# A fused attention and two-MLP kernel: sums of squares of the heads from one matmul pass instead of two, with squares paired across 64 partitions and stacked halves

## The chip, the cores and the metric

The kernel runs on one core of one Trainium2 chip. The metric is device time in microseconds (us). The engines are named as the profile names them: PE (matrix engine; PEld is its weight load), DVE (vector engine), ACT (scalar engine), POOL (GpSimd) and SP (the queue that issues all DMAs of this kernel).

## What is computed

The reference, cut to what matters:

```python
kv  = einsum('bhsd,bhse->bhde', k, v)            # 8 batches, 8 heads, 576 rows, head size 64
out = einsum('bhsd,bhde->bhse', q, kv)
rms = sqrt(mean(out * out, axis=-1) + 1e-06)     # over the 64 elements of one head
x   = out / rms * g_norm                         # -> 4608 tokens x 512
h   = x @ w_in                                   # 512 -> 2048
x   = (P(h) / (Q(h) + 1e-06)) @ w_out            # P cubic, Q quadratic in |h|; 2048 -> 512
y   = (silu(x @ w_gate) * (x @ w_val)) @ w_o2    # 512 -> 1536 -> 512
```

Everything is float32. The kernel gets float32 accuracy out of single-pass matmuls by splitting a factor into a rounded high part and the low rest.

## The kernel before

Tokens are worked on in nine tiles T = 0 to 8 of 512 tokens (`N`). Activations lie with features on partitions: one head pair (two heads of 64) fills 128 partitions, and four head pairs (`HP`) make the 512 features of a tile.

The first MLP is a loop over 144 steps s: nine tiles t of 16 slices f of the hidden layer. A step puts three kinds of work on PE: `h_mm(s)`, 12 matmuls of 512 columns (4 feature blocks, three products of high and low parts each, `mm3` on lines 112 to 114); `y_mm(s - 2)`, 12 matmuls of the second weight on the activation `ghl` of two steps before; and a piece of the attention of the next tile, `attn_pe(s)`. `g_step(s)` emits what the other engines do for a step: on ACT `e1`, `e2`, `e3` from the bank `ph`, then the high part of `ghl` of the step before, then two more functions of `e2`; on DVE two operations that finish the step before (`g_finish`), the products of this step, and at the end a list `lows` of subtractions that make low parts; on POOL the low part of `ghl`. `y_mm` begins with the high part and wants the low part at its second matmul (line 113).

The attention of tile T = t + 1 is spread over the 16 steps of tile t, four steps (phases 0 to 3, `ph` in the code) for each head pair. Phase 3 of the group before puts `out_mm` on PE (the output `po` in a bank). In phase 0 ACT squares `po` into `sq` (line 327). For T of 2 and more it also rounds the square to the high half of `sqhl` (line 330), and DVE subtracts at the end of the step to make the low half (put on the list by `attn_mid`). In phase 1, after `y_mm`, `ss_mm` sums the squares of each head over its partitions with a block matrix of ones: one matmul on the high half and one on the low half (lines 340 and 341). Phase 2 takes the reciprocal root on ACT and makes three DVE operations (`norm_ops`), phase 3 splits the result into `x` (ACT, then POOL). Tile T = 1 (worked on during t = 0) and tile T = 0 (worked on in a prologue ahead of the loop) use one unsplit matmul on line 338 instead.

Tiles T = 2 to 8 have 4 head pairs each: 28 groups of four steps, from about 143 to 790 us. After about 890 us the second MLP runs; it has no part in the change.

During the prologue and t = 0 the weights are fetched as 64-bit words and converted. `wa_fetch` takes one set per step: a slice of `w_in` and a slice of `w_out`, each 512 KB and one DMA (line 182), into one of two raw buffers that it takes in turn. `wa_scale` (ACT, end of a step) rescales both as soon as they have landed, DVE joins them in the next step, ACT and DVE split them, and the end of that frees the buffer for the fetch after the next. In the same steps SP issues the loads of k and v (`kv_load`) and of q. All instructions of an engine run in the order in which they are written (the schedule is written out by hand); DMAs are issued by SP in that order.

Of the kernel before, what the change touches and what calls it, by code (L numbers as in the profile page):

```python
# [8 lines left out]
F32 = mybir.dt.float32  # L9
F32R = mybir.dt.float32r  # L10
I32 = mybir.dt.int32
I64 = mybir.dt.int64
AF = mybir.ActivationFunctionType
ALU = mybir.AluOpType

P = 128
# [4 lines left out]
N = 512  # L21
# [3 lines left out]
HP = H // 2  # L25
# [16 lines left out]
def fused_kernel(ctx: ExitStack, tc: tile.TileContext, kv_main, kv_left, q_t, w_in, w_out, w_gate, w_val, w_o2, ab, g_norm, out):  # L42
# [13 lines left out]
    nc = tc.nc  # L56
# [15 lines left out]
    at_p = attn_ctx.enter_context(tc.tile_pool(name="attn", bufs=1, side="right"))  # L72
# [4 lines left out]
    ones = const.tile([P, P], F32R, name="ones")  # L77
    ones_f = const.tile([P, P], F32, name="ones_f")
    ones_b = const.tile([P, P], F32, name="ones_b")
    na = const.tile([P, 4], F32, name="na")  # L80
    rows = w_p.tile([1, 3, P], F32, tag="w3", name="rows")
# [7 lines left out]
    kvc = at_p.tile([P, B - 2, HP, D], F32, name="kvc")  # L89
    for n in (18, 20, 22, 24, 26, 28, 3):  # L90
        w_p.tile([P, 2, N], F32, tag=f"w{n}", name="place")
    kvf = w_p.tile([P, 2, HP, P], F32, tag="w31", name="kvf")

    def act(out, in_, func=AF.Copy, **kw):
        nc.scalar.activation(out=out, in_=in_, func=func, **kw)  # L95
# [34 lines left out]
    def w_exp(st):  # L130
        _, _, hf = w_views(st)
        act(hf, hf, AF.Prelu, scale=2.0 ** -112, alpha=-(2.0 ** 32))
# [33 lines left out]
    wa_src = [("i", f, w_in[f]) for f in range(LAG)]  # L166
    wa_sets = [(f,) for f in range(LAG)]
    for f in range(NF1):
        n = len(wa_src)
# [7 lines left out]
    def wa_fetch():  # L177
        if wa_n[0] < len(wa_sets):
            ns, (pool, tag) = wa_sets[wa_n[0]], wa_raw[wa_home[wa_n[0]]]
            r = pool.tile([P, 2 if tag in ("hl", "stg") else 1, N], I64, tag=tag, name="wraw")  # L180
            for j, n in enumerate(ns):
                nc.sync.dma_start(out=r[:, j, :], in_=wa_src[n][2])
            raws.append((ns, r[:, :len(ns), :].rearrange("p a n -> p (a n)")))
            wa_n[0] += 1

# [45 lines left out]
    st = {}  # L231
    segs = {}
    for t in range(TILES):
        t0, ss = t * N, []
        while t0 < (t + 1) * N:
            b = t0 // S
            n = min((b + 1) * S, (t + 1) * N) - t0
# [42 lines left out]
    def diag(j):  # L280
        return slice(64 * j, 64 * j + 64)

    def kv_evac_first(b, ps, hps):
        for j in range(2):
            dst, src = kvf[diag(j), b, hps, diag(j)], ps[diag(j), hps, diag(j)]
            act(dst, src)

    def kv_evac(n, k, ps):
        flat = kvc.rearrange("p b h d -> p (b h) d")
# [3 lines left out]
    def kv_split(b):  # L293
        hi, lo = kvh[b % 2], kvl[b % 2]
        ops = []
        for j in range(2):
            o = (diag(j), slice(0, HP), diag(j))
            src = kvf[diag(j), 1, :, diag(j)] if b == 1 else kvc[diag(j), b - 2, :, :]
            act(hi[o], src)
            ops.append(partial(sub, nc.vector if b < 3 else nc.gpsimd, lo[o], src, hi[o]))  # L300
        return ops

    def q_load(T, hp, pool=None, tag="q"):
# [21 lines left out]

    def square(T, ps):
        sq = at_p.tile([P, N], F32, tag="t1", name="sq")
        act(sq, ps, AF.Square)
        if T >= 2:
            hl = at_p.tile([P, 2, N], F32R, tag="hl", name="sqhl")  # L330
            act(hl[:, 0, :], sq)
            st["sql"] = (hl[:, 1, :], sq, hl[:, 0, :])
            return hl
        return sq

    def ss_mm(T, sq, ps):
        if T < 2:
            nc.tensor.matmul(ps, lhsT=ones_b, rhs=sq, start=True, stop=True)
        else:
            nc.tensor.matmul(ps, lhsT=ones, rhs=sq[:, 0, :], start=True, stop=False)  # L340
            nc.tensor.matmul(ps, lhsT=ones, rhs=sq[:, 1, :], start=False, stop=True)
        return ps

    def norm_start(T, pss, bufs=None):
# [5 lines left out]
    def norm_ops(ps, pss):  # L350
        r, u = st["n"]
        return [
            partial(stt, u, pss, D * EPS_RMS, u, ALU.add, ALU.mult),
            partial(stt, r, u, 3.0 * D, r, ALU.subtract, ALU.mult),
            partial(stt, u, ps, g_neg, r, ALU.mult, ALU.mult),
        ]

    def x_attn(T, hp, lo_eng, lows=None):
        if hp % 2 == 0:
            x_t[T, hp // 2] = x_p.tile([P, 2, 2, N], F32R, tag=f"x{T % 2}{hp // 2}", name="x")  # L360
        split(x_t[T, hp // 2][:, hp % 2, :, :], st["n"][1], lo_eng, lows)
# [12 lines left out]
    def at(c):  # L374
        T, f = divmod(c, NF1)
        i, ph = divmod(f, 4)
        return (T + 1, i, ph) if T + 1 < TILES else (None, None, None)

    def attn_head(c):

        T, i, ph = at(c)
        if ph == 0:
            st["sq"] = square(T, st["po"])
        elif ph == 2 and T >= 2:
            norm_start(T, st["ss"])

    def attn_start(c):
        T, i, ph = at(c)
        if T == 1 and ph == 1:
            norm_start(T, st["ss"])  # L390
        elif ph == 3 and T != 1:
            x_attn(T, i, nc.gpsimd)

    def attn_mid(c, lows):
        T, i, ph = at(c)
        if ph == 0 and T is not None and T >= 2:
            lows.append(partial(sub, nc.vector, *st["sql"]))
        elif T == 1 and ph == 2:
            x_attn(T, i, None, lows)
        return norm_ops(st["po"], st["ss"]) if ph == (1 if T == 1 else 2) else []  # L400

    def attn_tail(c):
        T, i, ph = at(c)
        if T is None:
            return
        f = c % NF1
        if c >= NF1 and f == 13 and T + 1 < B:
            run(kv_split(T + 1), 2)
        n = (T - 1) * HP + i + 1
        Tn, hp = n // HP + 1, n % HP  # L410
        if Tn < TILES:
            if ph == 0:
                q_load(Tn, hp)
            if ph == 2 and Tn > 1 and T > 1:
                q_split(Tn, hp)
# [44 lines left out]
    def run(ops, k=1):  # L460
        for op in ops[:k]:
            op()
        del ops[:k]

    def g_finish(s, ops, his=()):
        if s not in mid:
            return []
        e1, e2, e3 = mid.pop(s)
        stt(e1, e1, 1.0 + EPS_Q, e2, ALU.add, ALU.mult)
        stt(e3, e3, na[:, 0:1], e2, ALU.add, ALU.mult)  # L470
        run(ops, len(ops))
        w = s in WHOLE
        hl = g_p.tile([P, N] if w else [P, 2, N], F32 if w else F32R, tag="g", name="ghl")
        stt(hl if w else e3, e1, 2.0, e3, ALU.subtract, ALU.mult)
        lows = [hi() for hi in his[:1]]
        if not w:
            split(hl, e3, nc.gpsimd)
        hl_t[s] = hl
        return lows + [hi() for hi in his[1:]]

    def g_step(s, joins=(), his=(), exps=(), acts=()):
        ps = ew.pop(s)
        if s:
            attn_head(s)
        e1 = e_p.tile([P, N], F32, tag="e1", name="e1")
        e2 = e_p.tile([P, N], F32, tag="e2", name="e2")
        e3 = e_p.tile([P, N], F32, tag="e3", name="e3")
        act(e1, ps, AF.Square)
        act(e2, ps, AF.Abs, scale=ab_raw[:, 4:5])
        act(e3, ps, AF.Identity, scale=na[:, 3:4], bias=na[:, 2:3])  # L490
        if not s:
            attn_head(s)
        for r in exps:
            w_exp(r)
        attn_start(s)
        lows = [op for a in acts for op in a() or ()]
        ops = list(joins)
        lows = g_finish(s - 1, ops, his) + lows
        run(ops, len(ops))
        ops = attn_mid(s, lows)  # L500
        if s < NF1:
            run(ops)
        stt(e1, e1, b_abs[:, 1:2], e2, ALU.mult, ALU.add)
        act(e2, e1, AF.Abs_reciprocal_sqrt, bias=bias_q)
        act(e2, e2, AF.Square)
        nc.vector.tensor_tensor(out=e3, in0=e3, in1=ps, op=ALU.mult)
        run(ops)
        stt(e3, e3, na[:, 1:2], ps, ALU.add, ALU.mult)
        run(ops, len(ops))
        run(lows, len(lows))  # L510
        mid[s] = (e1, e2, e3)
# [527 lines left out]
    with tc.manual_schedule():  # L1039
# [8 lines left out]
        for i in range(HP):  # L1048
            kv_load(1)
            q_load(0, i, w_p, f"w{20 + i}")  # L1050
            if i == 0:
                nc.sync.dma_start(out=rows[:, 0, :], in_=g_norm.rearrange("(o p) -> o p", o=1))
                nc.sync.dma_start(out=rows[:, 2, :6], in_=ab.rearrange("(o p) -> o p", o=1))
            elif i == 1:
                wa_fetch()
# [4 lines left out]
        nc.vector.memset(rows[:, 1, :], 1.0)  # L1060
        nc.vector.memset(kvf, 0.0)
        nc.vector.memset(ones_b, 0.0)
        for j in range(2):
            nc.vector.memset(ones_b[diag(j), diag(j)], 1.0)
        nc.vector.memset(bias_q, 1.0 + EPS_Q)
        nc.vector.tensor_copy(out=ones, in_=ones_b)
        for i in range(2):
# [138 lines left out]
        for s in range(S1):  # L1206
# [62 lines left out]
            if t == TILES - 1:  # L1269
# [12 lines left out]
                elif 8 <= f < 12:  # L1282
                    k, c = divmod(f - 8, 2)
# [82 lines left out]
        for j in range(UP):  # L1366
            f, n = UP + j, 12 + 10 * j
# [19 lines left out]
        for n, i in enumerate(made):  # L1387
            at = (
# [3 lines left out]
            )[n % 3]  # L1392
# [88 lines left out]
```

## Time and profile before

| | before |
|---|---|
| time, median of 3 runs | 1680.99 us (1679.74 to 1682.69) |
| span of the profiled execution | 1678.3 us |
| PE busy | 1666.0 us (99%) |
| DVE busy | 1371.2 us (82%) |
| ACT busy | 1073.6 us (64%) |
| POOL busy | 473.1 us (28%) |
| granted TensorE clock, mean | 1.000 |

The span runs from the first to the last instruction of the profiled execution; its time by the clock of the runs is not told, and the median of the runs lies 2.7 us above the span. Busy time counts what an engine executes; it is not idle between overlapping matmuls. The TensorE clock was granted in full in every slice of the span.

### The profile page before, as it was taken

To read this page: it belongs to the slowest core of one execution; us is meant where nothing else is said; L and a number is where in the kernel's file an instruction comes from. 1 tells how busy PE (TensorE), PEld (TensorE's weight loads), DVE (VectorE), ACT (ScalarE), POOL (GpSimd) and SP (SyncE) were. 2 spreads that over 40 slices of the span, in tenths; PEclk is the share of its full clock that TensorE was granted. 3 is DMA by queue.
4 is the path that set the end of the run, shared out by engine and by line. 5 is a ranking of instruction groups with operands and counts; after the bars stand their busy time and mean duration, and the time that the engine had idled before them with its cause. 6 is when DMAs were issued, how large, how long until landed. Compare 5 with 4: busy or idle time off the path is not lost.

```text
span 1678.3 us, 24096 instructions
## 1 busy us (share of the span) xinstructions
PE 1666.0 (99%) x9040; PEld 1415.8 (84%) x9040; DVE 1371.2 (82%) x1913; ACT 1073.6 (64%) x1801; POOL 473.1 (28%) x331
## 2 busy tenths in 40 slices
PE   8999999999999999999999999999999999999999
PEld 5777888888888888888888888888888889999999
DVE  7999999999999999998996766778568859776665
ACT  7898888788788787877775444445435455444442
POOL 2112333333333343333330112223202155222221
PEclk9999999999999999999999999999999999999999
DMA  8861011011111110111425237243494354434431
GB/s 338 319 240 50 8 51 63 26 57 44 57 39 69 45 63 20 45 57 63 151 75 182 82 107 281 64 144 107 152 334 151 130 176 144 164 133 151 151 129 61
DMA packets 77850, 198.18 MB, mean 118 GB/s; under 512 B 6947, under 2 KB 35876, under 8 KB 75044
## 3 DMA queue, kind: packets, MB, share of 16 engines
q1 hardware_dynamic: 77732, 196.64, 33.3%
q8 instruction: 71, 1.16, 0.3%
q14 instruction: 47, 0.39, 0.1%
HBM read 130.02 MB, written 66.06 MB: 117 GB/s over the span
## 4 chain that ended last, share of the span: by engine, by line
PE 92%; DVE 4%; ACT 2%; DMA 2%; issue 1%; POOL 0%; SPq 0%; DVEq 0%; POOLq 0%; ACTq 0%
PE pb L112 10%; PE pb L113 10%; PE pb L114 10%; PE y L113 7%; PE ph L113 7%; PE ph L114 7%; PE ph L112 7%; PE y L114 7%; PE y L112 7%; PE pb L948 5%; PE pb L947 5%; PE pb L946 5%; DVE e L108 1%; ACT e L95 1%; DMA wraw<-in_w_in 1%
## 5 line engine op out<-in xcount | busy, mean ns | idle before, releaser
L98 POOL TENSOR_TENSOR ghl<-e,ghl 128x512 fp32r<-128x512 f32 x141 | 183.3, 1300 | 499.4 <-ACT ghl L95 289.8
L112 PE MATMUL pb<-xc,wu 128*128 128x512 f32 (+1 forms) x804 | 303.9, 378 | 0.0
L113 PE MATMUL pb<-xc,wu 128*128 128x512 f32 (+1 forms) x804 | 303.8, 378 | 0.0
L114 PE MATMUL pb<-xc,wu 128*128 128x512 f32 (+1 forms) x804 | 303.8, 378 | 0.0
L95 ACT ACTIVATE e<-pb 128x512 f32<-128x512 f32 (+1 forms) x162 | 92.8, 573 | 238.0 <-PE pb L114 237.7
L108 DVE SCALAR_TENSOR_TENSOR e<-e,e 128x512 f32<-128x512 f32 x285 | 226.3, 794 | 12.0 <-ACT e L95 4.9
L515 DVE TENSOR_TENSOR e<-e,pb 128x512 f32<-128x512 f32 (+1 forms) x216 | 140.6, 655 | 114.4 <-PE pb L114 63.5
L112 PE MATMUL ph<-x,wt 128*128 128x512 f32 x576 | 226.5, 393 | 0.3 <-ACT x L95 0.3
L113 PE MATMUL ph<-x,wt 128*128 128x512 f32 x576 | 225.0, 391 | 1.8 <-POOL x L98 1.6
L114 PE MATMUL ph<-x,wt 128*128 128x512 f32 x576 | 224.7, 390 | 0.0
L113 PE MATMUL y<-ghl,wt 128*128 128x512 f32 x564 | 221.5, 393 | 3.0 <-POOL ghl L98 2.8
L112 PE MATMUL y<-ghl,wt 128*128 128x512 f32 x564 | 221.5, 393 | 0.0
L114 PE MATMUL y<-ghl,wt 128*128 128x512 f32 x564 | 219.9, 390 | 0.0
L947 PE MATMUL pb<-wo,xo 128*128 128x256 f32 x756 | 213.9, 283 | 0.0
L948 PE MATMUL pb<-wo,xo 128*128 128x256 f32 x756 | 213.9, 283 | 0.0
L946 PE MATMUL pb<-wo,xo 128*128 128x256 f32 x756 | 213.9, 283 | 0.0
L112 PEld LDWEIGHTS pb<-xc,wu 128*128 128x128 f32 x804 | 151.0, 188 | 28.6 <-ACT e L95 0.4
L114 PEld LDWEIGHTS pb<-xc,wu 128*128 128x128 f32 x804 | 151.0, 188 | 28.1
L113 PEld LDWEIGHTS pb<-xc,wu 128*128 128x128 f32 x804 | 151.0, 188 | 28.0
L95 ACT ACTIVATE xo<-graw 128x768 fp32r<-128x768 f32 x122 | 99.1, 840 | 109.3 <-issue 49.9
L95 ACT ACTIVATE e<-ph 128x512 f32<-128x512 f32 x144 | 85.8, 596 | 119.3 <-PE ph L114 118.4
L946 PEld LDWEIGHTS pb<-wo,xo 128*128 128x128 f32 x756 | 145.1, 192 | 0.1
(138 smaller groups left out, 3409.2 us busy)
## 6 DMA issues: line engine op xcount, KB each, us to landing
graw<-gd SPq DMA_DIRECT2D x36, 768.0 KB, 4.4
gd<-gout SPq DMA_DIRECT2D x96, 256.0 KB, 2.2
kvm<-in_kv_main SPq DMA_DIRECT2D x32, 512.0 KB, 7.1
yraw<-yd SPq DMA_DIRECT2D x22, 512.0 KB, 7.0
q<-in_q_t SPq DMA_DIRECT2D x36, 256.0 KB, 3.7
yd<-sb SPq DMA_DIRECT2D x18, 512.0 KB, 3.5
out<-sb SPq DMA_DIRECT2D x17, 512.0 KB, 3.0
wraw<-in_w_in SPq DMA_DIRECT2D x16, 512.0 KB, 4.3
```

Source lines behind the costliest of these rows:

```text
L95: nc.scalar.activation(out=out, in_=in_, func=func, **kw)
L98: eng.tensor_tensor(out=out, in0=a, in1=b.bitcast(F32), op=ALU.subtract)
L108: nc.vector.scalar_tensor_tensor(out=out, in0=in0, scalar=scalar, in1=in1, op0=op0, op1=op1)
L112: nc.tensor.matmul(ps, lhsT=wh, rhs=xh, start=first, stop=False, skip_group_check=more)
L113: nc.tensor.matmul(ps, lhsT=wh, rhs=xl, start=False, stop=False, skip_group_check=more)
L114: nc.tensor.matmul(ps, lhsT=wl, rhs=xh, start=False, stop=last, skip_group_check=more)
L515: eng.tensor_tensor(out=out, in0=a, in1=b, op=op)
L946: nc.tensor.matmul(ps, lhsT=x[:, 0, i, :], rhs=wh, start=start, stop=False, skip_group_check=not first)
L947: nc.tensor.matmul(ps, lhsT=x[:, 0, i, :], rhs=wl, start=False, stop=False, skip_group_check=not first)
L948: nc.tensor.matmul(ps, lhsT=x[:, 1, i, :], rhs=wh, start=False, stop=stop, skip_group_check=not first)
```

## The change

The feature order inside a head pair is changed from (head, 64 elements) to (half, head, 32 elements): partitions 0 to 31 hold the first half of head 0, 32 to 63 the first half of head 1, 64 to 95 the second half of head 0, 96 to 127 the second half of head 1. A square and the square 64 partitions above it then belong to the same head. For tiles T of 2 and more:

- `square` makes two ACT squares of 64 partitions each, both written to partitions 0 to 63, and a POOL addition of the two in place of the rounding.
- `square_hi`, called by the new `attn_late` after the last function of `e2` in the same step, rounds the 64-partition sum to the high half in partitions 0 to 63 of `sqhl`; DVE writes the low half to partitions 64 to 127 at the end of the step.
- `ss_mm` is one matmul over all 128 partitions.

The matrix of ones follows the order (four fills instead of two), as do the evacuations of k times v (`kv_evac_first`, `kv_split`), the row of `g_norm`, and the rows of `w_in`: each slice is fetched with four DMAs of 32 partitions (128 KB) instead of one of 128 partitions.

```diff
--- before.py
+++ after.py
@@ -179,7 +179,13 @@
             ns, (pool, tag) = wa_sets[wa_n[0]], wa_raw[wa_home[wa_n[0]]]
             r = pool.tile([P, 2 if tag in ("hl", "stg") else 1, N], I64, tag=tag, name="wraw")
             for j, n in enumerate(ns):
-                nc.sync.dma_start(out=r[:, j, :], in_=wa_src[n][2])
+                if wa_src[n][0] == "o":
+                    nc.sync.dma_start(out=r[:, j, :], in_=wa_src[n][2])
+                else:
+                    src = wa_src[n][2].rearrange("p k n -> p (k n)")
+                    for k in range(4):
+                        at = 32 * (2 * (k % 2) + k // 2)
+                        nc.sync.dma_start(out=r[32 * k:32 * k + 32, j, :], in_=src[at:at + 32])
             raws.append((ns, r[:, :len(ns), :].rearrange("p a n -> p (a n)")))
             wa_n[0] += 1
 
@@ -280,10 +286,15 @@
     def diag(j):
         return slice(64 * j, 64 * j + 64)
 
+    def apart(ap, j):
+        return ap.rearrange("p i (h a e) -> p i h a e", h=2, a=2)[:, :, :, j, :]
+
+    def near(ap):
+        return ap.rearrange("p i (h e) -> p i h e", h=2)
+
     def kv_evac_first(b, ps, hps):
         for j in range(2):
-            dst, src = kvf[diag(j), b, hps, diag(j)], ps[diag(j), hps, diag(j)]
-            act(dst, src)
+            act(apart(kvf[diag(j), b, hps, :], j), near(ps[diag(j), hps, diag(j)]))
 
     def kv_evac(n, k, ps):
         flat = kvc.rearrange("p b h d -> p (b h) d")
@@ -294,10 +305,10 @@
         hi, lo = kvh[b % 2], kvl[b % 2]
         ops = []
         for j in range(2):
-            o = (diag(j), slice(0, HP), diag(j))
-            src = kvf[diag(j), 1, :, diag(j)] if b == 1 else kvc[diag(j), b - 2, :, :]
-            act(hi[o], src)
-            ops.append(partial(sub, nc.vector if b < 3 else nc.gpsimd, lo[o], src, hi[o]))
+            hj, lj = apart(hi[diag(j)], j), apart(lo[diag(j)], j)
+            src = apart(kvf[diag(j), 1], j) if b == 1 else near(kvc[diag(j), b - 2])
+            act(hj, src)
+            ops.append(partial(sub, nc.vector if b < 3 else nc.gpsimd, lj, src, hj))
         return ops
 
     def q_load(T, hp, pool=None, tag="q"):
@@ -325,20 +336,26 @@
 
     def square(T, ps):
         sq = at_p.tile([P, N], F32, tag="t1", name="sq")
-        act(sq, ps, AF.Square)
-        if T >= 2:
-            hl = at_p.tile([P, 2, N], F32R, tag="hl", name="sqhl")
-            act(hl[:, 0, :], sq)
-            st["sql"] = (hl[:, 1, :], sq, hl[:, 0, :])
-            return hl
+        if T < 2:
+            act(sq, ps, AF.Square)
+            return sq
+        up = at_p.tile([P, N], F32, tag="t2", name="up")
+        act(sq[diag(0)], ps[diag(0)], AF.Square)
+        act(up[diag(0)], ps[diag(1)], AF.Square)
+        nc.gpsimd.tensor_tensor(out=sq[diag(0)], in0=sq[diag(0)], in1=up[diag(0)], op=ALU.add)
         return sq
+
+    def square_hi():
+        sq = st["sq"][diag(0)]
+        hl = st["sq"] = at_p.tile([P, N], F32R, tag="hl", name="sqhl")
+        act(hl[diag(0)], sq)
+        st["sql"] = (hl[diag(1)], sq, hl[diag(0)])
 
     def ss_mm(T, sq, ps):
         if T < 2:
             nc.tensor.matmul(ps, lhsT=ones_b, rhs=sq, start=True, stop=True)
         else:
-            nc.tensor.matmul(ps, lhsT=ones, rhs=sq[:, 0, :], start=True, stop=False)
-            nc.tensor.matmul(ps, lhsT=ones, rhs=sq[:, 1, :], start=False, stop=True)
+            nc.tensor.matmul(ps, lhsT=ones, rhs=sq, start=True, stop=True)
         return ps
 
     def norm_start(T, pss, bufs=None):
@@ -393,11 +410,15 @@
 
     def attn_mid(c, lows):
         T, i, ph = at(c)
-        if ph == 0 and T is not None and T >= 2:
-            lows.append(partial(sub, nc.vector, *st["sql"]))
-        elif T == 1 and ph == 2:
+        if T == 1 and ph == 2:
             x_attn(T, i, None, lows)
         return norm_ops(st["po"], st["ss"]) if ph == (1 if T == 1 else 2) else []
+
+    def attn_late(c, lows):
+        T, i, ph = at(c)
+        if ph == 0 and T >= 2:
+            square_hi()
+            lows.append(partial(sub, nc.vector, *st["sql"]))
 
     def attn_tail(c):
         T, i, ph = at(c)
@@ -503,6 +524,7 @@
         stt(e1, e1, b_abs[:, 1:2], e2, ALU.mult, ALU.add)
         act(e2, e1, AF.Abs_reciprocal_sqrt, bias=bias_q)
         act(e2, e2, AF.Square)
+        attn_late(s, lows)
         nc.vector.tensor_tensor(out=e3, in0=e3, in1=ps, op=ALU.mult)
         run(ops)
         stt(e3, e3, na[:, 1:2], ps, ALU.add, ALU.mult)
@@ -1049,7 +1071,7 @@
             kv_load(1)
             q_load(0, i, w_p, f"w{20 + i}")
             if i == 0:
-                nc.sync.dma_start(out=rows[:, 0, :], in_=g_norm.rearrange("(o p) -> o p", o=1))
+                nc.sync.dma_start(out=rows[:, 0, :].rearrange("o (h a e) -> o h a e", h=2, a=2), in_=g_norm.rearrange("(o a h e) -> o h a e", o=1, a=2, h=2))
                 nc.sync.dma_start(out=rows[:, 2, :6], in_=ab.rearrange("(o p) -> o p", o=1))
             elif i == 1:
                 wa_fetch()
@@ -1060,8 +1082,9 @@
         nc.vector.memset(rows[:, 1, :], 1.0)
         nc.vector.memset(kvf, 0.0)
         nc.vector.memset(ones_b, 0.0)
-        for j in range(2):
-            nc.vector.memset(ones_b[diag(j), diag(j)], 1.0)
+        for k in range(4):
+            c = ones_b[32 * k:32 * k + 32].rearrange("p (h a e) -> p h a e", h=2, a=2)
+            nc.vector.memset(c[:, :, k % 2, :], 1.0)
         nc.vector.memset(bias_q, 1.0 + EPS_Q)
         nc.vector.tensor_copy(out=ones, in_=ones_b)
         for i in range(2):
```

## Rows read from the trace of the kernel before

**Rows 1.** The page: busy us (share of the span) by engine.

```profile
PE 1666.0 (99%) x9040; PEld 1415.8 (84%) x9040; DVE 1371.2 (82%) x1913; ACT 1073.6 (64%) x1801; POOL 473.1 (28%) x331
```

**Rows 2.** Windows: PE, PEld, DVE, ACT, POOL busy us (count), PEclk, DMA share, GB/s.

```profile
60.00:90.00 30.00, 29.30 (x295) 23.14 (x295) 29.55 (x44) 26.49 (x45) 5.18 (x4) 1.00 0.92 340
...
300.00:500.00 200.00, 199.96 (x901) 165.21 (x900) 187.18 (x257) 160.80 (x272) 72.09 (x57) 1.00 0.14 47
```

**Rows 3.** Windows again, one group of four steps, the one with the busiest DVE.

```profile
152.26:175.45 23.19, 23.19 (x105) 19.27 (x104) 22.12 (x31) 19.18 (x33) 7.93 (x6) 1.00 0.16 57
```

**Rows 4.** All waits of PE from 143 to 790 us: total, times, longest.

```profile
PE y L113 <- POOL ghl L98: 0.9, 1, 0.9
```

**Rows 5.** Chain of work from 370 us: start, us, what.

```profile
384.09 0.23 PE ss L341
```

**Rows 6.** Groups by line and form: xcount | busy us, mean ns | idle before.

```profile
L341 PE MATMUL ss<-sqhl,ones 128*128 128x512 f32 x28 | 11.0, 394 | 0.0
L95 ACT ACTIVATE sq<-po 128x512 f32<-128x512 f32 x36 | 21.0, 584 | 1.4 <-PE po L318 1.2
L95 ACT ACTIVATE sqhl<-sq 128x512 fp32r<-128x512 f32 x28 | 17.7, 633 | 0.9
L98 DVE TENSOR_TENSOR sqhl<-sq,sqhl 128x512 fp32r<-128x512 f32 x28 | 26.9, 960 | 0.0
L98 POOL TENSOR_TENSOR ghl<-e,ghl 128x512 fp32r<-128x512 f32 x141 | 183.3, 1300 | 499.4 <-ACT ghl L95 289.8 <-issue 130.3 <-PE y L114 40.4
L98 POOL TENSOR_TENSOR wo<-wraw,wo 128x256 fp32r<-128x256 f32 x5 | 3.8, 757 | 18.9 <-ACT wo L95 18.9
L98 POOL TENSOR_TENSOR kvl<-kvc,kvh 64x256 fp32r<-64x256 f32 x10 | 10.0, 1004 | 2.2 <-ACT kvh L95 1.9
```

**Rows 7.** Timeline around one phase 0: start, us, engine line op [idle before <-releaser].

```profile
394.99 1.28 POOL L98 TENSOR_TENSOR x<-u,x 128x512 fp32r<-128x512 f32 x1 [1.83 <-ACT x L95]
395.00 1.82 DVE L108 SCALAR_TENSOR_TENSOR e<-e,e 128x512 f32<-128x512 f32 x1
...
399.43 0.63 ACT L95 ACTIVATE sqhl<-sq 128x512 fp32r<-128x512 f32 x1
399.55 0.74 DVE L108 SCALAR_TENSOR_TENSOR e<-e,na,e 128x512 f32<-128x512 f32 x1
400.33 0.69 DVE L108 SCALAR_TENSOR_TENSOR e<-e,e 128x512 f32<-128x512 f32 x1
402.44 1.30 POOL L98 TENSOR_TENSOR ghl<-e,ghl 128x512 fp32r<-128x512 f32 x1 [3.52 <-ACT ghl L95]
402.95 0.63 ACT L95 ACTIVATE e<-e 128x512 f32<-128x512 f32 x1
404.21 0.68 DVE L108 SCALAR_TENSOR_TENSOR e<-e,e 128x512 f32<-128x512 f32 x1
404.57 0.60 ACT L95 ACTIVATE e<-ph 128x512 f32<-128x512 f32 x1 [0.98 <-PE ph L114]
404.59 0.39 PE L113 MATMUL y<-ghl,wt 128*128 128x512 f32 x1
407.09 0.39 PE L340 MATMUL ss<-sqhl,ones 128*128 128x512 f32 x1
```

**Rows 8.** Timeline of one weight fetch in t = 0, SP and ACT.

```profile
55.76 0.33 SPq L182 DMA_DIRECT2D wraw<-in_w_in  x1
56.14 1.15 SPq L182 DMA_DIRECT2D wraw<-in_w_out  x1
...
62.42 1.20 ACT L95 ACTIVATE wraw<-wraw 128x1024 f32<-128x1024 f32 x1 [0.33 <-DMA wraw<-in_w_out]
```

**Rows 9.** Timeline of the prologue: the first weights come in.

```profile
10.83 0.43 DVE L136 TENSOR_SCALAR wraw<-wraw 128x512 int32<-128x512 int32 x1 [1.70 <-DMA wraw<-in_w_in]
```

**Rows 10.** The page, DMA issues: xcount, KB each, median us to landing.

```profile
wraw<-in_w_in SPq DMA_DIRECT2D x16, 512.0 KB, 4.3
wraw<-in_w_out SPq DMA_DIRECT2D x16, 512.0 KB, 6.2
```

## The prediction, made before the changed kernel was run

> **What bounds the kernel now.** I read the page first: PE is busy 99% of the span, and DVE comes next [rows 1]. A share over the whole span says little about the stage that the change touches, so I went to the windows: between 300 and 500 us PE stands idle for 0.04 us of 200, DVE for 12.8 us (200 less 187.2) [rows 2]. The waits of PE from 143 to 790 us agree: one, of 0.9 us, for POOL's low part of `ghl` [rows 4]. So in the 28 groups PE sets the time, and work taken from it shortens the span, as long as nothing else becomes late. DVE is the candidate. A group lasts about 23.2 us, so 12.8 us in 200 are 1.49 us of idle DVE for a group; in the busiest group it is 1.07 us (23.19 less 22.12) [rows 3]. Earlier, in t = 0, nothing has room: of 30 us PE is busy 29.3, DVE 29.6, ACT 26.5, and the DMA engines 92% of the time [rows 2].
>
> **What is removed.** One matmul on `sqhl` for each of 28 groups. It shows as 394 ns [rows 6], but matmuls overlap; on the chain it holds 0.23 us [rows 5]. 28 times 0.23 is 6.4 us, all of it in the PE-bound stage. The second square, 0.58 us, takes the place of the rounding, 0.63 us, ahead of `e1` [rows 6]: nothing gained or lost there. No row shows a PSUM read that is written to other partitions; I take the square's own 0.58 us for it, for 64 partitions as for 128.
>
> **What is added in a group.** One POOL addition, one more ACT operation, and a DVE subtraction that waits for it. I worked this through for the group of rows 7. The second square ends where the rounding ended, at about 400.1. The addition then wants to start. What it costs DVE is shown by the POOL subtraction at 394.99: DVE's product of two SBUF operands beside it took 1.82 us instead of 0.69 [rows 7]. At 399.55 DVE has such an operation, which ends at about 400.3; POOL then has the turn and DVE's operation of 400.33 starts some 1.25 us later. (Beside a shorter or a waiting operation it would cost less; the lower bound is nothing.) The new rounding on ACT stands behind the last function of `e2`. That one starts at 402.95 now; DVE's operations ahead of it are late, so it starts near 403.6, and the rounding runs from about 404.2 to 404.8. The subtraction, the last of the step on DVE, waits for it and ends near 405.5, so DVE's next operation begins 1.2 us later than 404.21. (The subtraction takes 0.96 us on average now [rows 6], since many run beside POOL; here it falls clear of POOL, and I gave it the 0.69 us of its neighbours.)
>
> Who is late then? `ss_mm` wants the subtraction at 407.09 [rows 7]: 1.6 us are left. Behind the addition on POOL stands the `ghl` of the step, now 402.44 to 403.74; its ACT half slips by about 0.5 us, and PE wants it at 404.59: 0.35 us are left. Behind the rounding on ACT, which waits for POOL's addition, stands `e1` of the next step; it waits for PE until 404.57 anyway and would start near 404.8. Behind the subtraction stands all that DVE has to do. The 1.2 us must then be recovered from the group's own idle DVE time, 1.49 less the 0.23 that PE gains: 1.26 us. On average it just fits; in the busiest group (1.07 less 0.23) it lacks 0.36 us, which becomes a stall there or is handed on to the next group. I take 0.5 us for all stalls of the stage. Bounds: nothing, or the addition at a higher price. POOL's nearest rows are 128x512 at 1.30 us and, for 64 partitions, 64x256 at 1.00 us where 128x256 took 0.76 [rows 6]. I take 1.30, since the operands here are contiguous as in that row; the other end is 1.30 times 1.00/0.76, that is 1.7 us.
>
> **The weights in four pieces.** SP's issues of the two slices of a fetch stand 0.38 us apart [rows 8]. Three more pieces put `w_out`, and all that SP issues behind it (k, v, q), 1.15 us later. ACT's rescaling takes both slices together, and it starts where `w_out` lands: in rows 8 it waited 0.33 us for it. `w_out` takes 6.2 us to land against 4.3 for `w_in` [rows 10], which says that it stands behind other transfers part of the time; then a later issue is hidden. Bounds: below, nothing (the queue is the limit); above, each of the two raw buffers is refilled every second step, so 1.15 us stretch a step by 0.57, and some 12 steps by 6.9 us. A late rescaling first eats ACT's own slack, 3.5 us in 30 [rows 2], which is 0.8 us a step at about four steps in 30 us; that puts me near the lower end: +1.3 us.
>
> [...] No row shows a transfer onto 32 partitions. [...]
>
> In the prologue the first slice is awaited: DVE sat idle 1.70 us until it landed [rows 9]. SP has issued long before the landing, so pieces should cost little there: between 0 and the 1.15 us of the issues, I take 0.3. The strided evacuations move as much as before, the row of `g_norm` is still one DMA, and the two more fills of the ones lie ahead of the 1.70 us in which DVE idles [rows 9], which they would have to outgrow first: nothing.
>
> **The sum.** -6.4 + 0.5 + 1.3 + 0.3 = -4.3 us. Against the profiled execution the span goes from 1678.3 to about 1674.0; I carry the difference to the median of the runs, 2.7 us above it: 1680.99 - 4.3 = 1676.7 us.
>
> **The rivals.** *DVE takes over* (the side of slower). If the addition costs 1.7 us instead of 1.30, DVE is late by 1.2 + 0.4 = 1.6 us in each group. The point that decides is 1.49, the idle DVE time now: beyond it, a group is longer than before. 0.11 us over, 28 times, is +3.1; with weights and prologue +4.7: 1685.7. For it: the 64-partition row; DVE at 94% in the stage. Against: that row is of strided operands and may hold waits for DVE. Chance 0.12.
>
> *The gain is eaten by stalls.* The 1.2 us lateness meets tight groups such as rows 3; if half of the groups lack 0.36 us, 14 times 0.36 are 5.0 us: -6.4 + 5.0 + 1.6 = +0.2, 1681.2. PE would then wait for POOL's `ghl`. For it: the single PE wait today is just that one [rows 4]. Against: lateness may pass from a tight group to the next. Chance 0.15.
>
> *The weights come late.* [...] For it: t = 0 is full on every engine. Chance 0.15, half of it beyond the time at which slower begins.
>
> [...]
>
> *It does not do what it says*: a copy or a wait that I overlook keeps PE from closing up, and the time stays, 1681; chance 0.03. The forecast keeps 0.55.
>
> **How the numbers follow.** A measurement of this kernel can tell about 0.2% (3.4 us) from no change. Faster by more than that, below 1677.6: the forecast, 0.55. Within: stalls 0.15, half of the weights 0.08, no effect 0.03, together 0.26. Slower, above 1684.4: DVE 0.12 and the rest of the weights 0.07, 0.19. The low end is the whole 6.4 us with nothing lost and the subtractions off POOL's way: 1674.0. The high end takes in the upper bound of the weights and most of DVE's rival: 1685.5.
>
> **What would show it.** Right: 28 fewer matmuls on `sqhl`; the distance between two `ss` matmuls of groups shorter by 0.23 us; POOL additions of about 1.3 us; DVE busy at 94 to 97% between 300 and 500 us, and PE still idle for under 1 us there. The prediction is wrong if PE shows waits for `ghl` of several us between 143 and 790 (DVE took over), or if the first `ss` on `sqhl`, at 152 us now, comes more than 3 us later (weights).

## The result, and the profile after

The changed kernel took 1698.64 us (median of 4 runs, 1693.82 to 1703.08) against 1680.37 us before (median of 4 runs; 1680.99 was that of the first three): a ratio of 1.0104, 95% interval 1.0081 to 1.0127. It is slower by 18.3 us, where 4.3 us less had been forecast. The profiled execution is the quickest of the four; its span is 1692.0 us, 13.7 us more than that of before. The median lies 4.8 us above it, and no trace divides that part.

The page of the changed kernel gives busy us and shares of the span by engine, as rows 1 did. The granted clock, 0.998 on average, fell in two short stretches that the last section shows.

```profile
PE 1669.4 (99%) x9012; PEld 1410.7 (83%) x9012; DVE 1393.9 (82%) x1915; ACT 1096.9 (65%) x1829; POOL 520.7 (31%) x359
```

PE has its 28 matmuls less (9012 against 9040), and is still busy for 99%. The page cannot show where 13.7 us went: PE counts as busy about as long as before, though it has fewer matmuls. The windows can: the columns are those of rows 2 (busy us of PE, PEld, DVE, ACT, POOL, then clock, DMA share, GB/s).

```profile
30.00:60.00 30.00, 28.82 (x290) 22.20 (x291) 28.17 (x41) 25.56 (x44) 3.86 (x3) 1.00 1.02 319
60.00:90.00 30.00, 28.70 (x264) 22.39 (x262) 29.73 (x43) 26.92 (x46) 5.17 (x4) 1.00 1.01 315
...
300.00:500.00 200.00, 198.18 (x882) 161.22 (x881) 190.82 (x255) 166.39 (x279) 84.72 (x64) 1.00 0.12 43
```

In the 60 to 90 us window the DMA engines are now busy all the time and move 315 GB/s; they moved 340 at a share of 0.92 [rows 2]. In the 200 us of the groups PE idles for 1.8 us where it was 0.04, and DVE is busy for 3.6 us more.

To divide the loss I set windows from the first to the last of the 28 `ss` matmuls on `sqhl`. The first line is the kernel before, the second the changed one.

```profile
152.26:778.21 625.95, 625.84 (x2797) 517.40 (x2796) 581.47 (x798) 503.74 (x852) 223.33 (x173) 1.00 0.14 47
```

```profile
161.40:792.04 630.64, 625.79 (x2770) 510.45 (x2769) 601.10 (x799) 524.84 (x878) 268.42 (x199) 1.00 0.14 47
```

The first such matmul comes at 161.40 instead of 152.26 us: 9.1 us are lost ahead of the groups. Step 0 tells how they divide; its first `ph` matmul, before and then changed:

```profile
18.83 0.79 PE L112 MATMUL ph<-x,wt 128*128 128x512 f32 x1
```

```profile
20.86 0.79 PE L112 MATMUL ph<-x,wt 128*128 128x512 f32 x1
```

So 2.0 us are lost in the prologue and 7.1 us in t = 0. The 27 distances between groups add up to 630.64 instead of 625.95 us: 4.7 us more, where 27 times 0.23 less was forecast. Together 13.8 us, which is the whole difference of the two profiled executions. Per group that is 23.36 us after 23.18.

The waits name who made PE late in the groups (view of all waits, 143 to 800 us: total, times, longest):

```profile
PEld y L113 <- POOL ghl L98: 15.3, 27, 1.3
DVE sqhl L98 <- ACT sqhl L95: 13.1, 22, 0.6
PE y L113 <- POOL ghl L98: 5.3, 9, 0.9
DVE e L108 <- ACT e L95: 5.2, 25, 0.2
```

PE wants POOL's low part of `ghl` and its weight load stands for 15.3 us; before, that line had 3.7 us in the same stage. The 11.6 us more are about what was gained and lost again: 27 times 0.23, plus 4.7 on top, are 10.9. So both costs that the prediction took at little came at once, the weights and the lateness of DVE. The experiments separate them.

### The profile page after: what moved, and what is told of

It reads as the page before. It is cut to its first block, busy times and chain, and to the rows that moved or that the text cites. A ratio compares the mean times of both kernels' runs of the same rounds, so it can differ in the third digit from the quotient of the medians.

```text
span 1692.0 us, 24237 instructions
## 1 busy us (share of the span) xinstructions
PE 1669.4 (99%) x9012; PEld 1410.7 (83%) x9012; DVE 1393.9 (82%) x1915; ACT 1096.9 (65%) x1829; POOL 520.7 (31%) x359
## 5 line engine op out<-in xcount | busy, mean ns | idle before, releaser
L98 POOL TENSOR_TENSOR ghl<-e,ghl 128x512 fp32r<-128x512 f32 x141 | 187.1, 1327 | 454.3 <-ACT ghl L95 247.1
L108 DVE SCALAR_TENSOR_TENSOR e<-e,e 128x512 f32<-128x512 f32 x285 | 241.9, 849 | 10.9 <-ACT e L95 2.1
L95 ACT ACTIVATE ghl<-e 128x512 fp32r<-128x512 f32 x141 | 89.4, 634 | 92.8 <-DVE e L108 92.3
```

Source lines behind the costliest of these rows:

```text
L98: eng.tensor_tensor(out=out, in0=a, in1=b.bitcast(F32), op=ALU.subtract)
L108: nc.vector.scalar_tensor_tensor(out=out, in0=in0, scalar=scalar, in1=in1, op0=op0, op1=op1)
```

## The experiments

**Theory A:** two costs that have nothing to do with each other. Four DMAs for each slice of `w_in` make the start late; and in each group POOL's addition and the late rounding together make DVE later than it can recover. **Rival B:** one cost, the weights; the groups are slow only because they start out of step.

### The weights in one piece again

The rows of `w_in` are put in the new order in memory, so each slice is one DMA on 128 partitions as before; all else is the changed kernel.

```diff
-                if wa_src[n][0] == "o": ...   # four DMAs for a slice of w_in
+                nc.sync.dma_start(out=r[:, j, :], in_=wa_src[n][2])
...
-        "w_in": cols(moe_w_in),
+        "w_in": cols(moe_w_in.reshape(KD, 2, 2, 32, F1).transpose(0, 2, 1, 3, 4).reshape(DM, F1)),
```

> The changed kernel, but w_in lies in memory with its rows already in the new order, so that each slice is one DMA of 128 partitions again. Theory A (two costs: four DMAs for each slice of w_in make the start late by 9 us, and the 28 groups run 4.6 us longer instead of 6.4 us shorter): the first ss on sqhl comes at 152 us as before, the groups stay as in the changed kernel, the time is about 1685. Rival B (all of the loss comes from the weights, and the groups are only slow because they start late or out of step): about 1674.

Measured: 1686.3 us (1685.37 to 1687.93), ratio to before 1.0024 (1.0015 to 1.0034). The window over the 27 groups:

```profile
154.09:784.36 630.27, 625.99 (x2770) 510.47 (x2769) 600.77 (x799) 524.12 (x878) 267.31 (x199) 1.00 0.14 47
```

The groups still take 630.3 us, although they begin only 1.8 us later than before. Rival B falls: the groups cost 4.3 us by themselves. The time is 4.7 us above that of before on the same chip, so about 13.6 of the 18.3 us went with the DMAs. The page of this run also has a whole chain of work that ended last; its shares, first before, then here:

```profile
PE 92%; DVE 4%; ACT 2%; DMA 2%; issue 1%; POOL 0%; SPq 0%; DVEq 0%; POOLq 0%; ACTq 0%
```

```profile
PE 51%; DVE 32%; ACT 12%; issue 2%; DMA 1%; SPq 0%; POOL 0%; DVEq 0%; ACTq 0%; POOLq 0%
```

The chain has left PE for DVE and ACT: in the groups DVE now sets the time.

### The four DMAs alone, on neighbouring partitions and spread out

The kernel before, its slices of `w_in` fetched in four pieces of 32 neighbouring partitions:

```diff
+                    for k in range(4):
+                        at = 32 * k
+                        nc.sync.dma_start(out=r[32 * k:32 * k + 32, j, :], in_=src[at:at + 32])
```

> The kernel before, with nothing changed but that each slice of w_in is fetched by four DMAs of 32 neighbouring partitions. Theory A: the start is late by 9 us or more, the groups are as before: 1690 to 1697. Rival B' (the late start of the changed kernel comes from its strided evacuations and not from the DMAs): 1681.

Measured: 1693.94 us (1692.48 to 1695.69), ratio 1.0072 (1.0056 to 1.0087), 12.3 us more than before on the same chip. With the 4.7 us of the run with the weights in one piece that makes 17.0, which is near the 18.3 of the whole change (whose four runs spread over 9 us): the two costs add up.

The same number of DMAs of the same size, each on every fourth partition:

```diff
-                        at = 32 * k
-                        nc.sync.dma_start(out=r[32 * k:32 * k + 32, j, :], in_=src[at:at + 32])
+                        nc.sync.dma_start(out=r[k::4, j, :], in_=src[k::4])
```

> As the run with four DMAs of 32 neighbouring partitions, but each DMA takes every fourth partition, so it reaches all parts of the memory; number and size of the DMAs are the same. [...] If what costs is the number of DMAs (SP's issues, and the limit on those in flight): the same time as with neighbouring partitions, 1690 to 1697.

Measured: 1686.13 us (1684.04 to 1689.28), ratio 1.0023 (1.0013 to 1.0033). So 7.8 of the 12.3 us come from the neighbourhood of the pieces, and 4.5 stay with the number of DMAs. One thing goes with the partitions in this run: the spread pieces also read every fourth row of 4 KB from memory, where the others read 32 rows in a run. No run parts the two. The page's view of the DMA issues from 30 to 120 us (count, KB, median us to landing), first the neighbouring pieces, then the spread ones:

```profile
wraw<-in_w_in SPq DMA_DIRECT2D x40, 128.0 KB, 5.3
wraw<-in_w_out SPq DMA_DIRECT2D x10, 512.0 KB, 7.9
```

```profile
wraw<-in_w_in SPq DMA_DIRECT2D x44, 128.0 KB, 3.7
wraw<-in_w_out SPq DMA_DIRECT2D x11, 512.0 KB, 4.7
```

and the windows of both from 60 to 90 us, in the same order:

```profile
60.00:90.00 30.00, 28.32 (x240) 21.77 (x235) 29.30 (x41) 25.92 (x43) 5.14 (x4) 1.00 1.01 321
```

```profile
60.00:90.00 30.00, 28.61 (x292) 22.64 (x292) 28.98 (x42) 25.09 (x43) 5.19 (x4) 1.00 0.93 330
```

On neighbouring partitions the DMA engines have no idle time left and move 321 GB/s; spread, they do 330 at a share of 0.93, close to before. `w_out` lands 7.9 us after its issue instead of 4.7; it stands behind slower pieces. ACT's rescaling waited 13.3 us for `w_out` with the neighbouring pieces, 7.0 with the spread ones, 0.9 before (the view of waits up to 143 us). Why the neighbouring pieces are slower, no run shows.

What the number of DMAs does is seen at the start. This is SP's timeline of the changed kernel (start, us, engine, line, what; a line of several DMAs takes in the waits between them):

```profile
11.06 6.46 SPq L188 DMA_DIRECT2D wraw<-in_w_in  x8
17.71 0.35 SPq L183 DMA_DIRECT2D wraw<-in_w_out  x1
18.32 1.32 SPq L266 DMA_DIRECT2D kvm<-in_kv_main  x1
```

Eight pieces hold SP for 6.5 us, and the load of k and v behind them is issued at 18.32; the same load was issued at 10.82 in the trace of before. Between 9 and 18.4 us each of SP's issues follows by 0.02 to 0.09 us the landing of the DMA eight places ahead, as far as the trace tells the landings. The limit is the program's own: in both kernels each issue from the ninth on waits for the semaphore of the DMA eight places ahead, since eight semaphores are used in turn. So four pieces of 128 KB take four of eight places. One issue takes 413 ns in the median for a neighbouring piece and 592 for a spread one (view of the tile `wraw` up to 143 us); a whole slice took 328 before. The spread pieces cost SP more time than the neighbouring ones and the kernel is still faster, so the 7.8 us are, if anything, too little for the neighbourhood. How the 4.5 us divide between SP's time and the eight places was not tried apart.

### The rounding earlier

The run with the weights in one piece, and the rounding of the sum ahead of the two last functions of `e2` on ACT instead of behind them:

```diff
+        attn_late(s, lows)
         act(e2, e1, AF.Abs_reciprocal_sqrt, bias=bias_q)
         act(e2, e2, AF.Square)
-        attn_late(s, lows)
```

> As the run with the rows of w_in ordered in memory, and the rounding of the sum moved on ACT ahead of the two last functions of e2. In the changed kernel DVE's subtraction waited 13.1 us for that rounding in all. If this wait is the loss of the 28 groups: it is gone, and the time is 1674 to 1677. If the loss is that POOL's addition blocks DVE (one operation of DVE takes 1.67 instead of 0.69 us in each group): 1 to 3 us less than the run without the move, 1682 to 1684.

Measured: 1676.65 us (1675.93 to 1677.32), ratio to before 0.9971 (0.9959 to 0.9983): 9.7 us less than without the move, and faster than before. Its groups:

```profile
154.58:774.91 620.33, 620.22 (x2771) 512.10 (x2769) 601.41 (x799) 524.09 (x879) 268.02 (x199) 1.00 0.14 48
```

620.3 us: 5.6 less than before, nearly the 6.2 that 27 matmuls of 0.23 us give. DVE is busy as long as in the changed kernel (601.4 against 601.1 us), so POOL's addition still blocks it; only the wait for the rounding has gone. The block alone thus costs almost nothing. Taken by itself this says that the wait was the loss. The next two runs show that the wait alone costs nothing either.

### The addition left out, and the late rounding alone

The run with the weights in one piece, without the addition (the sums run over half of the squares only):

```diff
-        nc.gpsimd.tensor_tensor(out=sq[diag(0)], in0=sq[diag(0)], in1=up[diag(0)], op=ALU.add)
```

> As the run with the rows of w_in ordered in memory (1686.3 us), with POOL's addition left out: the sums are over half of the squares only, all other operations stay. DVE is no longer blocked by 1 us, but its subtraction still waits for the late rounding. If either lateness alone is small enough for the idle time of DVE to take up: 1676 to 1678, as much as the early rounding brought. If the wait for the rounding alone costs PE its gain: 1682 or more.

Measured: 1673.8 us (1673.55 to 1676.43), ratio 0.9961 (0.9946 to 0.9976): 7.2 us below the kernel before on its chip, where the run with the addition lies 4.7 above it on its own, so 11.9 us less, with the late rounding in place. The time is lower than expected by 2 us; its start is earlier than that of the run it is compared with (its first `ss` comes at 152.14 us, against 154.09).

The kernel before, with its rounding moved to the late place and nothing else:

```diff
-            act(hl[:, 0, :], sq)                  # in square
...
         act(e2, e2, AF.Square)
+        attn_late(s, lows)                        # rounds, and puts the subtraction on lows
```

> The kernel before, two matmuls on sqhl and no addition, with only the rounding of the squares moved behind the last function of e2, where the changed kernel has it. The subtraction then waits on DVE for ACT. If lateness at the end of phase 0 that exceeds what the next steps can recover is the cause: about 0.6 us of lateness with POOL not in the way is recovered, 1680 to 1683. If each 0.1 us of lateness costs PE at once: 28 times 0.6, above 1690.

Measured: 1681.42 us (1680.32 to 1682.91) against 1681.02, ratio 1.0004 (0.9994 to 1.0014): no change. Windows over the 27 groups, first without the addition, then the late rounding alone:

```profile
152.14:772.10 619.96, 619.80 (x2771) 512.26 (x2770) 579.78 (x798) 522.20 (x879) 232.33 (x172) 1.00 0.14 48
```

```profile
152.48:778.48 626.00, 625.89 (x2798) 517.44 (x2797) 574.36 (x799) 503.10 (x853) 224.04 (x172) 1.00 0.14 47
```

The waits for the rounding are there in both, and cost nothing (all waits from 143 to 800 us, in the same order):

```profile
DVE sqhl L98 <- ACT sqhl L95: 17.6, 23, 0.8
PEld y L113 <- POOL ghl L98: 4.2, 9, 1.2
```

```profile
DVE sqhl L98 <- ACT sqhl L95: 16.6, 23, 0.8
PEld y L113 <- POOL ghl L98: 3.7, 8, 1.2
```

DVE waits 16.6 and 17.6 us for the rounding, more than the 13.1 of the changed kernel, and PE does not notice. So neither the wait (these two runs) nor the block (the run before) is the cause alone: each is recovered within the group, both together are not. The theory of two causes for the two costs holds, with that addition; "the wait is the loss", which the run before suggested, does not.

### A better version

The early rounding with the row of `g_norm` in order in memory too, so that its DMA is one run:

```diff
-                nc.sync.dma_start(out=rows[:, 0, :].rearrange(...), in_=g_norm.rearrange(...))
+                nc.sync.dma_start(out=rows[:, 0, :], in_=g_norm.rearrange("(o p) -> o p", o=1))
```

> As the run with the early rounding (1676.65 us), and g_norm too lies in memory in the new order, so that its DMA is one run again: SP's issue of it took 0.76 us instead of 0.32 and all loads behind it are late. If that is the 0.9 us by which step 0 still starts late: about 1675.7. If it is not: 1676.6.

Measured: 1675.47 us (1674.94 to 1676.78), ratio 0.997 (0.9958 to 0.9981). It is 5.5 us faster than before on its chip, the run without it 5.0 on another: the difference lies within the intervals, and the first `ss` comes at 154.4 us, as there (154.6): not decided.

The same, with the addition on DVE ahead of `b_abs` instead of on POOL:

```diff
-        nc.gpsimd.tensor_tensor(out=sq[diag(0)], in0=sq[diag(0)], in1=up[diag(0)], op=ALU.add)
+        st["add"] = (sq[diag(0)], up[diag(0)])
...                                                  # in attn_mid
+        if ph == 0 and T >= 2:
+            s0, s1 = st["add"]
+            nc.vector.tensor_tensor(out=s0, in0=s0, in1=s1, op=ALU.add)
```

> As the run with the early rounding and g_norm in order, with the addition made by DVE (ahead of b_abs) and none by POOL. By the reading that POOL's addition blocks an operation of DVE for 0.98 us while DVE itself needs about 0.61: lateness falls by 0.4 us in a group, the last stalls go, 0.5 to 1 us less than with POOL, about 1675. If POOL's addition was free by now: up to 1 us more.

Measured: 1674.05 us (1672.98 to 1677.05), ratio 0.9963 (0.995 to 0.9976), the lowest median of the study for a kernel that does all the work. Its five runs overlap those of the run before, so the time alone does not part the two. Its groups:

```profile
155.97:775.58 619.61, 619.49 (x2771) 512.41 (x2769) 592.29 (x825) 519.35 (x879) 227.68 (x172) 1.00 0.14 48
```

They take 0.7 us less than with the early rounding and POOL's addition. A group lasts 619.61/27 = 22.95 us, 0.23 less than before: the whole matmul. DVE is busy for 592.3 us although it does the addition itself, 9.1 us less than when POOL does it (601.4). Against the run without an addition (579.8) the addition costs DVE 0.46 us in a group when it makes it, and 0.78 when POOL does (600.8).

## Why the prediction was wrong, step by step

**The matmul: right.** 0.23 us a group; the version with all of the gain shows exactly this. (The low end of the range, 1674.0, lies 0.6 us below 1680.99 - 6.4; nothing in the prediction gives that 0.6.)

**What one group adds to DVE: right.** Here is the changed kernel's group that answers to rows 7, from the timeline (start, us, what, idle before and its releaser):

```profile
409.92 0.57 ACT L95 ACTIVATE sq<-po 64x512 f32<-64x512 f32 x1
410.51 0.60 ACT L95 ACTIVATE up<-po 64x512 f32<-64x512 f32 x1
...
415.20 0.61 ACT L95 ACTIVATE sqhl<-sq 64x512 fp32r<-64x512 f32 x1
```

```profile
411.54 1.67 DVE L108 SCALAR_TENSOR_TENSOR e<-e,e 128x512 f32<-128x512 f32 x1
...
414.50 0.75 DVE L108 SCALAR_TENSOR_TENSOR e<-e,na,ph 128x512 f32<-128x512 f32 x1
415.85 0.69 DVE L98 TENSOR_TENSOR sqhl<-sq,sqhl 64x512 fp32r<-64x512 f32 x1 [0.60 <-PE ph L114]
416.57 0.69 DVE L108 SCALAR_TENSOR_TENSOR e<-e,e 128x512 f32<-128x512 f32 x1
```

```profile
411.25 1.41 POOL L345 TENSOR_TENSOR sq<-sq,up 64x512 f32<-64x512 f32 x1 [0.95 <-ACT up L95]
```

And of before, where rows 7 leave it out:

```profile
398.81 0.58 ACT L95 ACTIVATE sq<-po 128x512 f32<-128x512 f32 x1
403.21 1.08 DVE L98 TENSOR_TENSOR sqhl<-sq,sqhl 128x512 fp32r<-128x512 f32 x1
```

Counted from the first square (409.92 here, 398.81 before) DVE's next operation starts at 6.65 us instead of 5.40: 1.25 us late, where 1.2 had been worked out. The operation beside the addition takes 1.67 instead of 0.69, the rounding ends at 415.81 and the subtraction begins then. (The bracket names PE; the rounding that ended 0.04 us earlier is what it waited for.) The additions (ns, shortest, median, longest):

```profile
L345 POOL TENSOR_TENSOR sq<-sq,up x28: 1294/1303/1802, 154.3 to 785.2; 64x512 f32<-64x512 f32 x28
```

Most take the 1.30 us of the sum; seven of the 28 take 1.74 to 1.80, so the rival with an addition of 1.7 us was the case now and then. That is not the loss: in the run with the early rounding the additions take about as long (1.40 us on average, 1.42 here), and the gain is there.

**What a group can recover: wrong.** In the groups this is the step that failed: I took all idle time of DVE, 1.49 us a group, less the 0.23, as room for lateness, and 0.5 us for all stalls. The stalls took 11.0 us over 27 groups (630.64 less the 619.61 of the best version): 6.3 of gain lost (625.95 less 619.61) and 4.7 more. Not all idle time is room. In the changed kernel PE is late, so DVE ought to have none left, and yet it idles (630.64 - 601.10)/27 = 1.09 us a group. Of this 13.1/27 = 0.49 is the wait for the rounding, itself part of the lateness; 5.2/27 = 0.19 is a wait for `e2` from ACT, which runs late with DVE; and 0.41 are gaps too short for the view of waits, which the trace of before has too (0.40). The idle time of the kernel before is (625.95 - 581.47)/27 = 1.65 us over all groups. Less 0.41 and 0.19, 1.05 is room, and 0.82 after PE's own gain. A lateness of 1.25 then lacks 0.43 us a group; measured are 23.36 - 22.95 = 0.41. This agreement is no proof by itself, since all terms but the 1.25 are read from the traces whose lengths they explain. What bears it out are the 27 groups of four runs (us; DVE makes the addition in the last, the run above it leaves it out):

| | POOL's addition | no addition on POOL |
|---|---|---|
| rounding late | 630.27 | 619.96 |
| rounding early | 620.33 | 619.61 |

One lateness alone, 0.6 us of waiting or 0.7 us of more work for DVE (its busy time with POOL's addition), stays below 0.82 and costs under 0.8 us over all groups. The sum of the two, 1.2 us, does not, and costs 10.7.

I had named two rivals that this outcome answers to. "The gain is eaten by stalls" took half of the groups with 0.36 us; in the changed kernel 20 of the 27 are longer than in the best version, by 0.2 to 0.85 us. "DVE takes over" made a group longer than before once the lateness passes 1.49; with 1.05 in its place, 1.25 makes a group 0.20 us longer, and it is 0.17 (4.7/27). Both signs of being wrong came, PE's waits for `ghl` and the late first `ss`. The signs of being right did not tell the cases apart: 28 fewer matmuls, additions of 1.3 us and DVE at 95% between 300 and 500 us came as well.

**The weights: wrong.** The prediction took 1.3 us for t = 0 and 0.3 for the prologue; the profiled execution lost 7.1 and 2.0 us there, and the four DMAs alone cost 12.3 us in time. The mechanism of the upper bound (a later `w_out`, awaited by ACT) was at work: those waits grew from 0.9 to 13.3 us. Its 6.9 us were still too few, as they counted SP's issues alone. No row of before shows what slower transfers onto 32 partitions would add; the half of the third rival's chance that lies beyond 1684.4 rested on a value that no run shows. What the runs showed in its place is 5.3 us to landing for a neighbouring piece and 3.7 for a spread one. Two steps failed. One was "then a later issue is hidden", with ACT's slack to take up the rest: the spread pieces, with the DMA engines at 330 GB/s and a share of 0.93, still cost 4.5 us. The other was to leave slower transfers out of the sum: the DMA engines were 92% busy [rows 2], the transfers became slower, and the queue had nothing left to hide them in, 7.8 us by the runs with neighbouring and spread pieces. The loads of k and v behind the pieces, which I named and did not price, were late as well; PE waited for one:

```profile
24.47 0.69 PE L280 MATMUL pkv<-kvm 128*64 128x64 f32 x16 [2.36 <-DMA kvm<-in_kv_main]
```

## What to carry to other kernels

Before counting on the idle time of the second-busiest engine, take out what cannot be moved: the short gaps between its operations (0.41 us a group here), and waits that run late together with it (0.19); two small latenesses in the same step that are free one by one can cost the whole gain together (here under 0.8 us each over 27 groups, and 10.7 together). A reordering of rows that splits a load into blocks of neighbouring partitions belongs in the layout in memory, or in pieces spread over the partitions, when the DMA engines are near full: here, at a share of 0.92, neighbouring pieces cost 12.3 us and spread ones 4.5. An addition on POOL beside DVE's operations on two SBUF operands cost DVE 0.78 us a group here, and 0.46 us when DVE made it itself.

## What the runs showed of the hardware

PE's granted clock fell twice in the changed kernel, after stretches in which PE had waited. The windows around the first: PE is busy 1.8 of 4 us, then waits for a load of k and v until 24.47, and from 26.0 to 29.4 the granted clock is 0.50.

```profile
20.00:24.00 4.00, 1.82 (x5) 0.87 (x5) 3.90 (x7) 3.85 (x8) 1.23 (x2) 1.00 1.02 323
24.00:26.00 2.00, 1.53 (x23) 1.40 (x24) 1.97 (x3) 1.46 (x4) 2.00 (x2) 1.00 1.05 413
26.00:29.40 3.40, 3.40 (x18) 2.04 (x18) 3.37 (x5) 1.81 (x4) 1.93 (x2) 0.50 1.04 363
```

The second fall follows a stretch of 2 us in which PE was busy for 1.0:

```profile
99.00:101.00 2.00, 0.99 (x3) 0.48 (x3) 2.00 (x2) 1.97 (x4) 1.27 (x1) 1.00 1.01 346
101.00:104.50 3.50, 3.50 (x10) 2.72 (x9) 3.50 (x6) 2.91 (x5) 0.00 (x0) 0.51 1.02 342
```

The kernel before kept the full clock in its profiled execution (1.000 on average). Whether the waits brought the falls on was not shown; 3.4 us at half the clock can hold at most 1.7 us of work more, an estimate from the window above. The four DMAs are not needed for a fall: two runs with the weights in one piece had such stretches too, the early rounding one from 25.3 us and the one with the addition on DVE two, from 11.3 and 25.0 us, at a granted clock of 0.50 (0.999 and 0.998 on average over the span). In the profiled executions of the five runs with the weights in one piece the first `ss` comes anywhere between 152.1 and 156.0 us, so a difference of 2 us in the start of a single execution need not come from an edit; the price of the weights goes by the medians of the runs.

The subtraction writes to partitions 64 to 127, the operations around it to 0 and up. It ends at 416.54 and the next operation begins at 416.57; before, the next began at 404.21, 0.08 us ahead of the end of the subtraction that had started at 403.21. So it is in all 28 groups of either trace, 0.07 to 0.09 us ahead before and 0.02 to 0.03 us behind now: DVE's operations no longer overlap there, some 0.1 us a group. That the partitions are the cause was not shown.
